# A planner's costs, latencies and transfer model are exchanged in a gated linear attention + mixture-of-experts kernel

## Chip, cores, metric

One core of a Trainium2 chip. The metric is the device time of one execution in microseconds, as the median of several runs.

## What is computed

Two stages. The first is a gated linear attention over 4 batches, 8 heads, 768 steps and 48 features; the second is a mixture of 4 experts over its 3072 x 384 output.

```python
f = 1.0 / (1.0 + np.exp(-f_logit))
for t in range(768):
    state = f[:, :, t, :, None] * state + np.einsum('bhd,bhe->bhde', k[:, :, t], v[:, :, t])
    y[:, :, t] = np.einsum('bhd,bhde->bhe', q[:, :, t], state)
x = y.transpose(0, 2, 1, 3).reshape(3072, 384)
p = domain_probs / (domain_probs.sum(-1, keepdims=True) + 1e-09)
for e in range(4):                                  # w1[e]: 384 x 1024, w2[e]: 1024 x 384
    out += p[:, e:e + 1] * (np.maximum(x @ w1[e], 0.0) @ w2[e])
```

## The kernel before

**Tiling.** The 768 steps are cut into 6 slices (c = 0 to 5) of 128 steps. A slice holds 4 batch blocks (b), so 512 rows of x. Each slice goes through attention (per block) and then through the four experts (per slice).

**Attention of one block.** The steps, by the names that the planner gives them: `gate1` and `gate2` (ACT, L247 and L251: exp and ln of the gate's logits; two blocks at a time from slice 1 on); `cs` (PE, L255: running sum over time with a triangular matrix; in slice 0 also four one-column matmuls, L258); `exps` (ACT, L262 and L264: exp of the negative and of the positive sum, and in slice 0 the small `egs`, L266); `q` and `k` (L276: products with those exps, on DVE or POOL); `v` (a cast, L216 or L218). Then q and k are turned: in slices 0 and 1 by PE transposes (`tpq`, `tpk`, L285) and one PSUM copy (`ev_tp`, ACT or DVE), from slice 2 on by a DMA transpose (`tp`, L289). `at` (PE, L300) makes the scores, `ev_at0` and `ev_at1` (DVE, L304) mask them, `y` (PE, L311 and L315) applies them to v and to the state, `ev_y` copies the result, and `xt` turns it into the transposed input xT of the experts (slices 0 and 1: PE, L340, and a copy `ev_xt`; later: DMA, L293). `kv`, `ev_kv`, `state` (L321, L328, L335) carry the state to the next slice.

**Experts of one slice.** Eight `h` units for each expert (L344, three matmuls of 512 columns each), each followed by a `relu` (ACT L352 or DVE L350), and eight `o` units (L356, four matmuls of 384 columns), every second followed by an eviction `ev_o` (L363, L365 or L367). The h units of expert e are interleaved with the o units of expert e - 1. In slice 1 the first two experts are done in two halves of the rows (blocks 0 and 1, then 2 and 3), so that the first half can begin when its two blocks are there. The h units of slice 0 need all four blocks' xT and the first weight; from slice 2 on all four blocks of the slice's xT.

**Transfers.** Loads of q, k, v and f and all stores, transposes and small `egs` copies are issued by SP, in one order. The eight weight transfers (768 KB each) are issued by POOL (L229). Two waits are written out by hand: the first weight waits until the last k block of slice 0 has landed (L231), and the first load of slice 1 waits until the sixth weight (index 5) has landed (L225).

**What sets the order.** The kernel's text does not give an order of instructions. Each step is an `Op` with a cost for every engine that could do it, a priority, the steps that it depends on, and the buffers that it takes and frees. `Plan.run` (L58) plays the whole program in advance: whenever an engine is free, it takes the step of the best (lowest) priority whose inputs are ready and whose buffers can be had. Engines are asked in the order PE, ACT, DVE, POOL, DMA. The instructions are then emitted in the order of that play, so the plan fixes which engine does a step and what stands before it in each engine's queue; the waits in the program itself come from the data, not from the plan. A step is ready (L46) at the latest of its inputs' ends plus their `lag`, plus `LATENCY` if the input was made on another engine, or 0.05 if on the same one. Buffers are counted in `rooms` (L134): among them four PSUM banks for the experts and four for attention, three `e` buffers for the exps. "DMA" is one row in the plan: a load of one block holds it for 1.05 us, a weight for 4.5 us, and the data is there `lag` (2.0) later.

Priorities: slice 0's loads -1000 and up, weight issues -500 and up, slice 1's loads -400 and up, attention of slice 0 -200 + 3.6 b + 0.8 s with s the step's place in the chain (L501), expert units 0, 1, 2 ... in their order, relus 3 less than their unit, and attention of the next slice between the units (base + 2 + 5 b + s, L537). After the play, PE's idle time before the first h unit is filled with matmuls on a constant tile (`pad`, L551 and L556), one for each 0.2 us of idle time.

Of the kernel before, what the change touches and what calls it, by code (L numbers as in the profile page):

```python
# [14 lines left out]
class Op:  # L15


    def __init__(self, name, costs, emit, prio, deps=(), takes=(), frees=(), lag=0.0):
        self.name, self.costs, self.emit, self.prio = name, costs, emit, prio
        self.deps = [d for d in deps if d is not None]  # L20
        self.takes, self.frees, self.lag = list(takes), list(frees), lag
        self.end = self.start = self.engine = None
        self.pad = 0


class Plan:


    LATENCY = 0.2

    def __init__(self, rooms):
        self.ops, self.rooms = [], {r: list(range(n)) for r, n in rooms.items()}
        self.slot, self.left = {}, {}

# [23 lines left out]
    def run(self):  # L58
        for o in self.ops:
            for k in o.frees:  # L60
                self.left[k] = self.left.get(k, 0) + 1
        left = sorted(self.ops, key=lambda o: o.prio)
        free_at = {e: 0.0 for o in left for e in o.costs}
        free_at.update({"DMA": 0.8, "DVE": 5.0, "POOL": 3.5, "ACT": 2.1, "PE": 2.0})
        freeing, done, now = [], [], 0.0
        while left:
            for f in [f for f in freeing if f[0] <= now + 1e-9]:
                freeing.remove(f)
                self.rooms[f[1]].append(f[2])
            for e in ("PE", "ACT", "DVE", "POOL", "DMA"):  # L70
                while free_at[e] <= now + 1e-9:
                    for o in left:
                        if e in o.costs:
                            t = self.ready(o, e)
                            if t is not None and t <= now + 1e-9 and self.take(o):
                                break
                    else:
                        break
                    left.remove(o)
                    o.engine, o.start, o.end = e, now, now + o.costs[e]  # L80
                    free_at[e] = o.end
                    for k in o.frees:
                        self.left[k] -= 1
                        if self.left[k] == 0:
                            freeing.append((o.end + self.LATENCY, k[0], self.slot[k]))
                    done.append(o)
            nexts = [t for t in free_at.values()] + [f[0] for f in freeing]
            for o in left:
                for e in o.costs:
                    nexts.append(self.ready(o, e) or 0.0)  # L90
            nexts = [t for t in nexts if t > now + 1e-9]
            if left and not nexts:
                raise RuntimeError("no step can run: " + ", ".join(o.name for o in left[:8]))
            if left:
                now = min(nexts)
        return done
# [3 lines left out]
def kernel(  # L100
# [120 lines left out]
    def load(c, nm, b, n):  # L221
        ins[c, nm, b] = nc.sync.dma_start(out=tl(nm, c, b // 2)[:, hh(b, n), :],  # L222
                                          in_=srcs[nm][c, :, b * H:(b + n) * H, :])
        if (c, nm, b) == (1, "f", 0):
            after(ins[c, nm, b], ins["w", 5])  # L225
# [34 lines left out]
    def exps(c, b):  # L260
        cs, e = tl("cs", c, b), tl("e", c, b)
        nc.scalar.activation(out=e[:, 0].rearrange("t (d h) -> t h d", d=D), in_=cs[:, 0:HD].rearrange("t (i r d) -> t r i d", r=2, d=D),  # L262
                             func=AF.Exp, scale=-1.0)
        nc.scalar.activation(out=e[:, 1], in_=cs[:, 0:HD], func=AF.Exp)  # L264
        if c == 0:
            nc.scalar.activation(out=tl("egs", c, b), in_=cs[0:MP, HD:HD + NP], func=AF.Exp, scale=-1.0)  # L266
# [107 lines left out]
    ld = {}  # L374
    nw = [(0, 1), (1, 1), (0, 2), (2, 1), (1, 2), (3, 1), (2, 2), (3, 2)]

    def add_load(c, nm, b, n, prio, deps=()):
        op = P.add(f"ld {nm}{c}.{b}", {"DMA": 1.05 * n}, lambda e: load(c, nm, b, n), prio,
                   deps=deps, takes=[(nm, c, b // 2)], lag=2.0)
        for i in range(n):  # L380
            ld[c, nm, b + i] = op
        return op
# [4 lines left out]
    for i, (e, which) in enumerate(nw):  # L387
        iss = P.add(f"w issue {i}", {"POOL": 0.9}, lambda _, i=i, e=e, which=which: load_w(i, e, which),
                    -500 + i, deps=[ld[0, "k", B - 1]])
        wd[e, which] = wd[i] = P.add(f"w {i}", {"DMA": 4.5}, lambda _: None, -500 + (0, 1, 2, 3, 4, 5, 101.5, 103.5)[i], deps=[iss], lag=2.0)  # L390
    for half in range(2):
        for j, nm in enumerate("fkqv"):
            add_load(1, nm, 2 * half, 2, -400 + 4 * half + j, deps=[wd[5]])
# [4 lines left out]
    def attention(c, slot, gran):  # L398
# [10 lines left out]
        for b in range(B):  # L409
# [6 lines left out]
                       deps=[G[b]], takes=[pt_("cs")], lag=0.2, frees=[("gp", c, half)])  # L416
            ex = P.add(f"exps {c}.{b}", {"ACT": 0.98 if c else 1.1}, on(exps), s(0) + 0.1, deps=[cs],
                       takes=[("e", c, b)] + ([("egs", c, b)] if c == 0 else []), frees=[pt_("cs")])
            GS.append(P.add(f"egs {c}.{b}", {"DMA": 1.0}, on(dma_egs), s(3), deps=[ex], takes=[("egs", c, b)],
                            frees=[("e", c, b)], lag=2.0) if c and more else None)  # L420
            pe = {"DVE": 0.6, "POOL": 1.0} if c < 2 else {"POOL": 1.0}
            qm = P.add(f"q {c}.{b}", pe, one(product, 0), s(4) - 0.2,
                       deps=[ex, ld[c, "q", b]], takes=[("qk", c, b)], frees=[("q", c, half), ("e", c, b)])
            km = P.add(f"k {c}.{b}", pe, one(product, 1), s(4) - 0.1,
                       deps=[ex, ld[c, "k", b]], takes=[("qk", c, b)], frees=[("k", c, half), ("e", c, b)])
            vb = P.add(f"v {c}.{b}", {"ACT": 0.52, "DVE": 0.36} if c == 0 else {"POOL": 0.5, "ACT": 0.52} if c == 1 else {"POOL": 0.5}, one(cast_v), s(4),
                       deps=[ld[c, "v", b]], takes=[("vb", c, b)], frees=[("v", c, half)])
            if c < 2:
                tq = P.add(f"tpq {c}.{b}", {"PE": 0.22}, on(pe_tp, 0), s(4), deps=[qm],
                           takes=[pt_("tp")], frees=[("qk", c, b)], lag=0.2)  # L430
                tk = P.add(f"tpk {c}.{b}", {"PE": 0.22}, on(pe_tp, 1), s(4) + 0.01, deps=[km],
                           takes=[pt_("tp")], frees=[("qk", c, b)], lag=0.2)
                et = P.add(f"ev_tp {c}.{b}", {"DVE": 0.69, "ACT": 1.05}, lambda e, b=b: copy(e, tl("QK", c, b)[0:MP], tl("tp", c, b)), s(4) + 0.1,
                           deps=[tq, tk], takes=[("QK", c, b)], frees=[pt_("tp")])
            else:
                et = P.add(f"tp {c}.{b}", {"DMA": 1.8}, on(dma_tp), s(4), deps=[qm, km], takes=[("QK", c, b)],
                           frees=[("qk", c, b)], lag=2.2)
            at = P.add(f"at {c}.{b}", {"PE": 0.35}, on(pe_at), s(7), deps=[et],
                       takes=[pt_("A", 0), pt_("A", 1)], lag=0.2, frees=[("QK", c, b)])
# [3 lines left out]
                      takes=[pt_("y")], frees=[("QK", c, b), ("AT", c, b), ("vb", c, b)], lag=0.2)  # L443
# [4 lines left out]
            if c < 2:  # L448
                xt = P.add(f"xt {c}.{b}", {"PE": 0.17}, on(pe_xt), s(13), deps=[ey],
                           takes=[pt_("xp")], frees=[("yb", c, b)], lag=0.2)  # L450
                xdone[c, b] = P.add(f"ev_xt {c}.{b}", {"ACT": 0.48, "DVE": 0.4},
                                    lambda e, b=b: copy(e, tl("xT", c)[:, :, b * T:(b + 1) * T], tl("xp", c, b)),
                                    s(13) + 0.1, deps=[xt], takes=[("xT", c)], frees=[pt_("xp")])
            else:
                xdone[c, b] = P.add(f"xt {c}.{b}", {"DMA": 0.9}, on(dma_xt), s(13), deps=[ey], takes=[("xT", c)],
                                    frees=[("yb", c, b)], lag=2.2)
            X.append(xdone[c, b])
        for b in range(B if more else 0):
# [4 lines left out]
                       takes=[pt_("KV")], frees=[("vb", c, b), ("qk", c, b)], lag=0.2)  # L463
# [9 lines left out]
    def add_h(c, e, fc, n0, n1, xs):  # L473
# [3 lines left out]
                  deps=[wd[e, 1]] + [xdone[c, b] for b in xs], takes=[key], lag=0.2, frees=[("xT", c)])  # L477
# [5 lines left out]
    def add_o(c, e, nt, half):  # L483
# [8 lines left out]
                                  deps=d + [wd[e, 2], omm.get((c, e, nt))], takes=[key], lag=0.2, frees=[("h", c, e)])  # L492
        if half == 1 or by_cols:
# [4 lines left out]
            if e == E - 1:  # L498
                P.add(f"store {c}.{nt}.{part}", {"DMA": 0.6}, lambda _: store(c, nt, cols), p, deps=[ev], frees=[("o", c, nt)])
# [20 lines left out]
    for c in range(C):  # L520
        u0 = unit[0]
        pl = P.add(f"ld p{c}", {"DMA": 0.5}, lambda e, c=c: load_p(c), -900 if c == 0 else u0 - 6, lag=2.0)
# [15 lines left out]
        if c + 2 < C:  # L538
            for half in range(2):
                for j, nm in enumerate("fkqv"):  # L540
                    add_load(c + 2, nm, 2 * half, 2, u0 + 30 + 4 * half + j)
# [49 lines left out]
```

## Time and profile before

| what | value |
|---|---|
| median of 3 runs | 304.89 us (304.5, 304.89, 315.0) |
| the profiled execution, its own time | 304.54 us |
| its span in the profile | 302.7 us |
| granted TensorE clock, mean | 0.999 |
| PE busy | 293.2 us |
| ACT / DVE / POOL busy | 170.8 / 138.1 / 95.5 us |
| start of the first L344 matmul (expert stage of slice 0) | 22.74 us |
| HBM read / written | 31.51 / 4.72 MB |

The profile is of one execution; PE's busy time is a union of overlapping matmul records, so it tells that PE had work, not how fast it went. PE is TensorE's matmuls, PEld its weight loads, DVE VectorE, ACT ScalarE, POOL GpSimd, SP SyncE, SPq the issuing of DMAs on SP. A line of the timeline or of the chain gives a start and a duration in us, then engine, line of the code, output and input. The bracket behind it is the idle time of that engine before the instruction, and what ended it.

### The profile page before, as it was taken

To read this page: it belongs to the slowest core of one execution; us is meant where nothing else is said; L and a number is where in the kernel's file an instruction comes from. 1 tells how busy PE (TensorE), PEld (TensorE's weight loads), DVE (VectorE), ACT (ScalarE), POOL (GpSimd) and SP (SyncE) were. 2 spreads that over 40 slices of the span, in tenths; PEclk is the share of its full clock that TensorE was granted. 3 is DMA by queue.
4 is the path that set the end of the run, shared out by engine and by line. 5 is a ranking of instruction groups with operands and counts; after the bars stand their busy time and mean duration, and the time that the engine had idled before them with its cause. 6 is when DMAs were issued, how large, how long until landed. Compare 5 with 4: busy or idle time off the path is not lost.

```text
span 302.7 us, 5517 instructions
## 1 busy us (share of the span) xinstructions
PE 293.2 (97%) x2112; PEld 169.4 (56%) x2143; DVE 138.1 (46%) x273; ACT 170.8 (56%) x295; POOL 95.5 (32%) x157
## 2 busy tenths in 40 slices
PE   7899999999999999999999999999999999999995
PEld 5565555567775655455555555555555555555553
DVE  6774013787853764516555344544423443201223
ACT  5767654857865444676356475345566344475440
POOL 4584400409656237423426143522332100000000
PEclk9999999999999999999999999999999999999999
DMA  7999999954994589866997877301322201100003
GB/s 157 203 193 204 207 206 193 228 83 91 217 207 84 111 161 187 189 122 120 182 187 134 216 142 147 56 13 28 100 61 51 48 14 30 67 22 2 0 0 106
DMA packets 137355, 36.10 MB, mean 119 GB/s; under 512 B 128496, under 2 KB 135792, under 8 KB 137328
## 3 DMA queue, kind: packets, MB, share of 16 engines
q1 hardware_dynamic: 131568, 29.45, 49.1%
q0 software_dynamic: 5760, 6.29, 12.4%
q8 instruction: 17, 0.28, 0.4%
q14 instruction: 10, 0.08, 0.1%
HBM read 31.51 MB, written 4.72 MB: 120 GB/s over the span
## 4 chain that ended last, share of the span: by engine, by line
PE 88%; DMA 4%; DVE 2%; SPq 2%; issue 1%; POOL 1%; ACT 1%; DVEq 0%; ACTq 0%; POOLq 0%
PE ps_m L356 41%; PE ps_m L344 40%; DMA w_sb<-in_moe_w_dram 3%; PE ps_t L300 2%; SPq L222 2%; DMA f<-in_f_logit_dram 1%; PE ps_t L315 1%; PE ps_t L321 1%; PE ps_t L311 1%; PE ps_t L255 1%; PE ps_t L285 1%; DVE qk L276 1%; POOL qk L276 0%; DVE AT L304 0%; POOL Sf L335 0%
## 5 line engine op out<-in xcount | busy, mean ns | idle before, releaser
L352 ACT ACTIVATE h<-ps_m 128x512 bf16<-128x512 f32 (+1 forms) x171 | 98.3, 577 | 103.0 <-PE ps_m L344 92.9
L356 PE MATMUL ps_m<-w_sb,h 128*128 128x384 bf16 x776 | 153.0, 324 | 0.2
L344 PE MATMUL ps_m<-xT,w_sb 128*128 128x512 bf16 (+1 forms) x593 | 150.4, 362 | 2.1 <-DVE o L367 0.3
L356 PEld LDWEIGHTS <-h 128*128 128x128 bf16 x776 | 73.0, 98 | 57.0
L363 DVE SCALAR_TENSOR_TENSOR o<-ps_m,pn,o 128x384 f32<-128x384 f32 (+1 forms) x73 | 44.6, 611 | 96.8 <-PE ps_m L356 89.4
L344 PEld LDWEIGHTS <-w_sb 128*128 128x128 bf16 x624 | 59.8, 98 | 47.1 <-issue 0.7
L276 POOL TENSOR_TENSOR qk<-q,e 128x384 bf16<-128x384 f32 x19 | 22.8, 1204 | 64.9 <-ACT e L262 64.4
L304 DVE TENSOR_TENSOR AT<-ps_t,mask 128x512 bf16<-128x512 f32 x48 | 31.1, 683 | 19.2 <-PE ps_t L300 19.1
L335 POOL TENSOR_TENSOR Sf<-Sf,egs 48x192 f32<-48x192 f32 x40 | 20.4, 510 | 48.8 <-DVE Sf L328 46.8
L350 DVE TENSOR_SCALAR h<-ps_m 128x512 bf16<-128x512 f32 (+1 forms) x37 | 20.7, 572 | 22.0 <-PE ps_m L344 19.8
L276 POOL TENSOR_TENSOR qk<-k,e 128x384 bf16<-128x384 f32 x20 | 21.0, 1052 | 19.8 <-ACT e L264 12.9
L262 ACT ACTIVATE e<-ps_t 128x384 f32<-128x384 f32 x24 | 20.7, 864 | 3.7 <-PE ps_t L255 2.4
L328 DVE TENSOR_TENSOR Sf<-Sf,ps_t 48x192 f32<-48x192 f32 x40 | 14.0, 349 | 6.1 <-PE ps_t L321 5.3
L336 POOL CAST sb<-Sf 48x192 bf16<-48x192 f32 x40 | 13.6, 339 | 2.6
L365 ACT ACTIVATE o<-ps_m,pn 128x384 f32<-128x384 f32 x20 | 11.6, 580 | 3.9 <-PE ps_m L356 3.1
L264 ACT ACTIVATE e<-ps_t 128x384 f32<-128x384 f32 x24 | 13.0, 541 | 0.0
L556 PE MATMUL ps_m<-busy 128*128 128x256 bf16 x71 | 11.5, 301 | 1.3 <-DVE busy L140 1.3
L218 DVE CAST yb<-ps_t 128x384 bf16<-128x384 f32 x16 | 8.9, 555 | 7.4 <-PE ps_t L315 6.3
L247 ACT ACTIVATE ex<-f 128x768 f32<-128x768 f32 (+1 forms) x14 | 10.5, 748 | 3.1 <-DMA f<-in_f_logit_dram 2.9
L315 PE MATMUL ps_t<-vb,AT 128*128 128x48 bf16 x192 | 11.4, 184 | 0.7 <-DVE vb L218 0.7
L315 PEld LDWEIGHTS <-AT 128*128 128x128 bf16 x192 | 9.8, 97 | 3.0 <-issue 1.0
L251 ACT ACTIVATE gp<-ex 128x768 bf16<-128x768 f32 (+1 forms) x14 | 10.5, 751 | 0.4
(50 smaller groups left out, 139.9 us busy)
## 6 DMA issues: line engine op xcount, KB each, us to landing
w_sb<-in_moe_w_dram POOLq DMA_DIRECT2D x8, 768.0 KB, 18.8
out_dram<-o SPq DMA_DIRECT2D x23, 192.0 KB, 2.1
f<-in_f_logit_dram SPq DMA_DIRECT2D x10, 384.0 KB, 4.3
k<-in_k_dram SPq DMA_DIRECT2D x10, 384.0 KB, 5.2
q<-in_q_dram SPq DMA_DIRECT2D x10, 384.0 KB, 5.3
v<-in_v_dram SPq DMA_DIRECT2D x10, 384.0 KB, 5.5
f<-in_f_logit_dram SPq DMA_DIRECT2D x4, 192.0 KB, 4.0
k<-in_k_dram SPq DMA_DIRECT2D x4, 192.0 KB, 4.0
```

The costliest lines, as they stand in the source:

```text
L262: nc.scalar.activation(out=e[:, 0].rearrange("t (d h) -> t h d", d=D), in_=cs[:, 0:HD].rearrange("t (i r d) -> t r i d", r=2, d=D), func=A ...
L276: engines[eng].tensor_tensor(out=tl("qk", c, b)[:, j, :, 0:D].rearrange("t (i r) d -> t i r d", r=2), in0=tl("qk"[j], c, b // 2)[:, hh(b), ...
L304: nc.vector.tensor_tensor(out=tl("AT", c, b)[:, r].rearrange("s i t -> s (i t)"), in0=tl("A", c, b, r).rearrange("s i t -> s (i t)"), in1= ...
L315: nc.tensor.matmul(out=y[:, h * D:(h + 1) * D], lhsT=AT[:, r, i, :], rhs=vb[:, h, :], start=(c == 0), stop=True, skip_group_check=True)
L328: nc.vector.tensor_tensor(out=Sf[rows, b], in0=Sf[rows, b], in1=KV[rows, :, r, :], op=ALU.add)
L335: nc.gpsimd.tensor_tensor(out=Sf[rows, b], in0=Sf[rows, b], in1=eg, op=ALU.mult)
L336: nc.gpsimd.tensor_copy(out=nb[rows, b, :, r * D:(r + 1) * D], in_=Sf[rows, b])
L344: nc.tensor.matmul(out=tl("hp", c, e, fc, n0)[:, n0:n1], lhsT=w1_sb[:, e, kk, fc * 128:(fc + 1) * 128], rhs=tl("xT", c)[:, kk, n0:n1], sta ...
L350: nc.vector.tensor_relu(out=dst, in_=src)
L352: nc.scalar.activation(out=dst, in_=src, func=AF.Relu)
L356: nc.tensor.matmul(out=tl("op", c, e, nt, part)[:, cols], lhsT=tl("h", c, e)[:, fc, nt * T:(nt + 1) * T], rhs=w2_sb[:, e, fc, cols], start ...
L363: nc.vector.scalar_tensor_tensor(out=o, in0=op, scalar=pe, in1=o, op0=ALU.mult, op1=ALU.add)
```

## The change

No computation, buffer or transfer is added or removed, and the two waits written out by hand stay as they are. What changes is the play that sets the order:

- `LATENCY` goes from 0.2 to 0.07, and the `lag` of every PE step from 0.2 to 0.05. A step may be taken up to `AHEAD` = 0.06 us before it is ready (it then starts when it is ready).
- Transfers on SP get a model of a ring: a DMA costs its issue time on "DMA" (0.6 for a load, 1.2 to 1.25 for two `egs` copies or a transpose, 0.45 for a store), its data passes through one `ring` in order (1.0 for a block, 0.1 to 0.6 for the others), the issue is held back when the ring is more than 4.0 us behind, and the data is there 1.6 us after its turn in the ring.
- The weights leave "DMA" and get a row "W" of their own, in the order of issue, each 4.5 us, `lag` 1.5.
- In the plan slice 1's loads depend on weight 7 instead of weight 5, and the loads of slice c + 2 on the last v load of slice c + 1.
- `exps` becomes two steps (`exps0`, `exps1`) of 0.88 and 0.54 us (0.72 in slice 0) in place of one of 0.98 (1.1 in slice 0); `q` depends on the first, `k` on the second, `egs` on the first.
- Costs: products 0.7 on DVE and 1.2 or 1.1 on POOL (0.6 and 1.0 before); DVE is free from 5.2 on (5.0).

The diff, its core (the same `lag=0.2` to `0.05` edit is left out where it is repeated):

```diff
-    LATENCY = 0.2
+    LATENCY, AHEAD = 0.07, 0.06
...
-        free_at.update({"DMA": 0.8, "DVE": 5.0, "POOL": 3.5, "ACT": 2.1, "PE": 2.0})
+        free_at.update({"DMA": 0.8, "DVE": 5.2, "POOL": 3.5, "ACT": 2.1, "PE": 2.0})
...
-            for e in ("PE", "ACT", "DVE", "POOL", "DMA"):
+            for e in ("PE", "ACT", "DVE", "POOL", "DMA", "W"):
...
-                            if t is not None and t <= now + 1e-9 and self.take(o):
+                            if t is not None and t <= now + self.AHEAD and self.take(o):
...
-                    o.engine, o.start, o.end = e, now, now + o.costs[e]
+                    o.engine, o.start = e, max(now, t)
+                    o.end = o.start + o.costs[e]
+                    if o.ring is not None:
+                        self.ring = max(self.ring, o.end) + o.ring
+                        o.end = max(o.end, self.ring - 4.0)
+                        o.lag = self.ring - o.end + 1.6
...
-                            freeing.append((o.end + self.LATENCY, k[0], self.slot[k]))
+                            freeing.append((o.end + (self.LATENCY if o.ring is None else o.lag), k[0], self.slot[k]))
...
-    def exps(c, b):
+    def exps(c, b, j):
         cs, e = tl("cs", c, b), tl("e", c, b)
-        nc.scalar.activation(out=e[:, 0].rearrange("t (d h) -> t h d", d=D), in_=cs[:, 0:HD].rearrange("t (i r d) -> t r i d", r=2, d=D),
-                             func=AF.Exp, scale=-1.0)
-        nc.scalar.activation(out=e[:, 1], in_=cs[:, 0:HD], func=AF.Exp)
-        if c == 0:
+        if j == 0:
+            nc.scalar.activation(out=e[:, 0].rearrange("t (d h) -> t h d", d=D), in_=cs[:, 0:HD].rearrange("t (i r d) -> t r i d", r=2, d=D),
+                                 func=AF.Exp, scale=-1.0)
+        else:
+            nc.scalar.activation(out=e[:, 1], in_=cs[:, 0:HD], func=AF.Exp)
+        if j == 1 and c == 0:
             nc.scalar.activation(out=tl("egs", c, b), in_=cs[0:MP, HD:HD + NP], func=AF.Exp, scale=-1.0)
...
-        op = P.add(f"ld {nm}{c}.{b}", {"DMA": 1.05 * n}, lambda e: load(c, nm, b, n), prio,
-                   deps=deps, takes=[(nm, c, b // 2)], lag=2.0)
+        op = P.add(f"ld {nm}{c}.{b}", {"DMA": 0.6}, lambda e: load(c, nm, b, n), prio,
+                   deps=deps, takes=[(nm, c, b // 2)], ring=1.0 * n)
...
-        wd[e, which] = wd[i] = P.add(f"w {i}", {"DMA": 4.5}, lambda _: None, -500 + (0, 1, 2, 3, 4, 5, 101.5, 103.5)[i], deps=[iss], lag=2.0)
+        wd[e, which] = wd[i] = P.add(f"w {i}", {"W": 4.5}, lambda _: None, -500 + i, deps=[iss], lag=1.5)
...
-            add_load(1, nm, 2 * half, 2, -400 + 4 * half + j, deps=[wd[5]])
+            add_load(1, nm, 2 * half, 2, -400 + 4 * half + j, deps=[wd[7]])
...
-            ex = P.add(f"exps {c}.{b}", {"ACT": 0.98 if c else 1.1}, on(exps), s(0) + 0.1, deps=[cs],
-                       takes=[("e", c, b)] + ([("egs", c, b)] if c == 0 else []), frees=[pt_("cs")])
-            GS.append(P.add(f"egs {c}.{b}", {"DMA": 1.0}, on(dma_egs), s(3), deps=[ex], takes=[("egs", c, b)],
-                            frees=[("e", c, b)], lag=2.0) if c and more else None)
-            pe = {"DVE": 0.6, "POOL": 1.0} if c < 2 else {"POOL": 1.0}
+            ex = [P.add(f"exps{j} {c}.{b}", {"ACT": (0.88, 0.54 if c else 0.72)[j]}, on(exps, j), s(0) + 0.1 + 0.1 * j, deps=[cs],
+                        takes=[("e", c, b)] + ([("egs", c, b)] if c == 0 else []), frees=[pt_("cs")]) for j in range(2)]
+            GS.append(P.add(f"egs {c}.{b}", {"DMA": 1.2}, on(dma_egs), s(3), deps=[ex[0]], takes=[("egs", c, b)],
+                            frees=[("e", c, b)], ring=0.1) if c and more else None)
+            pe = {"DVE": 0.7, "POOL": 1.2} if c < 2 else {"POOL": 1.1}
...
-                et = P.add(f"tp {c}.{b}", {"DMA": 1.8}, on(dma_tp), s(4), deps=[qm, km], takes=[("QK", c, b)],
-                           frees=[("qk", c, b)], lag=2.2)
+                et = P.add(f"tp {c}.{b}", {"DMA": 1.25}, on(dma_tp), s(4), deps=[qm, km], takes=[("QK", c, b)],
+                           frees=[("qk", c, b)], ring=0.5)
...
-                xdone[c, b] = P.add(f"xt {c}.{b}", {"DMA": 0.9}, on(dma_xt), s(13), deps=[ey], takes=[("xT", c)],
-                                    frees=[("yb", c, b)], lag=2.2)
+                xdone[c, b] = P.add(f"xt {c}.{b}", {"DMA": 1.2}, on(dma_xt), s(13), deps=[ey], takes=[("xT", c)],
+                                    frees=[("yb", c, b)], ring=0.2)
...
-                P.add(f"store {c}.{nt}.{part}", {"DMA": 0.6}, lambda _: store(c, nt, cols), p, deps=[ev], frees=[("o", c, nt)])
+                P.add(f"store {c}.{nt}.{part}", {"DMA": 0.45}, lambda _: store(c, nt, cols), p, deps=[ev], frees=[("o", c, nt)], ring=0.6)
...
-        pl = P.add(f"ld p{c}", {"DMA": 0.5}, lambda e, c=c: load_p(c), -900 if c == 0 else u0 - 6, lag=2.0)
+        pl = P.add(f"ld p{c}", {"DMA": 0.6}, lambda e, c=c: load_p(c), -900 if c == 0 else u0 - 6, ring=0.5)
...
-                    add_load(c + 2, nm, 2 * half, 2, u0 + 30 + 4 * half + j)
+                    add_load(c + 2, nm, 2 * half, 2, u0 + 30 + 4 * half + j, deps=[ld[c + 1, "v", B - 1]])
```

## The prediction

> **What bounds the kernel now.** I read the page's busy line and chain first, then the chain of waits in order of time, then the timeline of the first 70 us engine by engine.
>
> ```profile
> span 302.7 us, 5517 instructions
> ...
> PE 293.2 (97%) x2112; PEld 169.4 (56%) x2143; DVE 138.1 (46%) x273; ACT 170.8 (56%) x295; POOL 95.5 (32%) x157
> ...
> PE 88%; DMA 4%; DVE 2%; SPq 2%; issue 1%; POOL 1%; ACT 1%; DVEq 0%; ACTq 0%; POOLq 0%
> ```
>
> The chain is PE for 88% of the span. In order of time it is PE from 22.74 us on; before that it is a weight transfer, released by a load:
>
> ```profile
> 13.03 1.36 POOL qk L276
> 14.38 0.25 issue
> 14.63 8.07 DMA w_sb<-in_moe_w_dram
> 22.70 0.05 issue
> 22.74 0.39 PE ps_m L344
> ```
>
> So the first MoE matmul (call it the start) waits for the first weight, issued 0.3 us after the last k block landed (14.32). But the other input, slice 0's xT, is ready only just before it. The timeline shows where its last block's (b=3) products were made:
>
> ```profile
> 13.53 0.55 ACT L264 ACTIVATE e<-ps_t 128x384 f32<-128x384 f32 x1
> ...
> 15.72 0.54 DVE L276 TENSOR_TENSOR qk<-k,e 128x384 bf16<-128x384 f32 x1
> 16.18 0.84 DVE L276 TENSOR_TENSOR qk<-q,e 128x384 bf16<-128x384 f32 x1
> ...
> 21.96 0.48 ACT L216 COPY xT<-ps_t 128x384 bf16<-128x384 bf16 x1 [0.73 <-PE ps_t L340]
> 22.74 0.98 PEld L344 LDWEIGHTS <-w_sb 128*128 128x128 bf16 x6 [0.55 <-DMA w_sb<-in_moe_w_dram]
> ```
>
> xT is whole at 22.44: cover of 0.3 us, no more. From the end of the products (17.02) to xT it took 5.42 us.
>
> After the start PE is nearly perfect: a unit (three L344 or four L356 matmuls) goes every 0.65 us. From the matmuls' start times I count two real holes, about 0.25 us at 69.55 and 0.5 us at 80.89. Slice 1 is the tight place. Its first load waits for the sixth weight and its chain runs from 52.29 to 66.76:
>
> ```profile
> 42.16 0.37 SPq L222 DMA_DIRECT2D f<-in_f_logit_dram  x1
> ```
>
> ```profile
> 52.29 0.84 ACT L247 ACTIVATE ex<-f 128x768 f32<-128x768 f32 x1 [1.30 <-DMA f<-in_f_logit_dram]
> ...
> 66.28 0.48 ACT L216 COPY xT<-ps_t 128x384 bf16<-128x384 bf16 x1 [1.62 <-PE ps_t L340]
> ```
>
> PE runs out of slice 0's units at 69.2, so slice 1's first half had 2.4 us to spare.
>
> **The change part by part.** No instruction is added or removed; each engine's order changes. The most to be won is therefore little: the start cannot pass the first weight (at most the 0.3 us between landing and issue), and behind it there are 0.75 us of holes. I follow the planner's rule by hand from the costs in the code to learn the order, and price that order with durations of the trace.
>
> *The start.* By the new costs slice 0's exps take 0.88+0.72 us on ACT where one step took 1.1; the trace has 0.87, 0.53 and 0.16 overlapping, about 1.25 in all. As two steps they can be parted, and ACT is asked before DVE. Working it through: ev_tp of b=0 goes to ACT (ready 8.53, ACT free 8.48; it was on DVE), so b=1's exps start at 9.58. v of b=0 goes to ACT at 14.32. POOL takes b=2's q at 14.39, then at 15.59 the eight weight issues (ready 15.07, best priority), planned to 22.79, so POOL is shut for b=3's products. exps1 of b=3 is set behind ev_xt of b=0, ev_tp of b=2 and v of b=2, to about 18.6; a near tie at 16.92 could put it at 16.9. Either way DVE gets k of b=3 behind the two masks of b=2, whose priority is better.
>
> Priced with the trace: on ACT, b=0's ev_tp runs 8.15 to 9.2 (1.02 us). Behind it wait b=1's exps, and for them POOL's and DVE's products. ev_tp of b=2 ends near 17.3; v of b=2 landed at 17.18 and is cast by 17.7 (0.51); exps1 of b=3 ends near 18.2, against 14.08. The masks of b=2 follow at about 18.0 to 19.3 (0.64 each), then k (0.54) to 19.8. With the same 5.42 us behind it xT is whole at 25.2: 25.2 - 22.74 = **+2.5 us**. Bounds: -0.3 (issue gap) and +3.5 (a PSUM bank still held by b=1's y when b=2's scores want two adds 0.6, a worse mix of copies 0.4). I take +2.5, the row-by-row sum. Nothing hides it: the weight's cover ends at 22.7 to 22.9.
>
> *Slice 1's loads.* In the plan they now depend on the eighth weight instead of the sixth; on SP they still wait only for the sixth (the wait in the load function is untouched), so data will land as before, f at 52.27. But ACT, DVE and PE get slice 1's steps where the plan has them. Before: loads and weights in one DMA row, 0.8 + 16 x 1.05 + 0.5 = 18.1, seven weights to 49.6, f's 2.1 and 2.2 to land: 53.9, for a start worked out at 25.05: 28.9 us after it. New: W begins at about 16.5, eight times 4.5 is 52.5, +1.57, +0.6 issue, +2.0 ring, +1.67: f at 58.4 for a start worked out at 26.2 in the same way, 32.2 after it. That is 3.3 us later in PE's stream. Against it six PE hand-overs in the chain cost 0.12 planned instead of 0.4 and six hand-overs back 0.07 instead of 0.2, 2.5 us less, with the dearer exps +0.9: net 1.6 less. Chain later by 1.7 us, spare 2.4: **0**. If the cover goes, it costs what exceeds 2.4. The second half gains: its f was planned 41.8 us after the start and is 40.2 now, so I let most of the 0.75 us of holes go: **-0.5** (bounds -0.75 and 0). Late next is then PE itself.
>
> The trace shows weights and loads sharing engines: that f took 10.1 us from issue to landing where the page's median is 4.3, and the eighth weight landed 5.25 us after the seventh, where the third to seventh came every 3.6 to 4.4. [...]
>
> *Tighter hand-overs.* From an h unit's first matmul to its relu the trace has 0.85 us (35.21 to 36.06): 0.645 + 0.205, planned 0.12 now, 0.4 before. A step chosen at its very first moment makes PE wait up to 0.1; with moments spread over a 0.65 us unit that is 0.1 x 0.1 / 1.3, 0.008 us a step, for some 300 steps at most 2 us, but PSUM banks and slots leave most of them room: **+0.2** (0 to 2).
>
> *Slices 2 to 5.* Attention there follows its slots; xT landed 2 to 3 us ahead of need (slice 4: 205.57 against about 208). DMA transposes are planned shorter (3.35 against 4.2 us), slice 2's loads at about 72 as before (71.23 in the trace). **0** (0 to +1). The tail behind the last matmul (299.6 to 302.7) keeps its instructions: 0.
>
> Sum: +2.5 + 0 - 0.5 + 0.2 = +2.2. The profiled execution ran 304.54 us (span 302.7 and 1.8 around it), 0.35 below the median of 304.89; 304.54 + 2.2 = 306.7, as a median 307.0.
>
> **The rivals.**
> 1. *The start stays, slice 1 stalls.* If b=3's products come in time, the start is at 22.8 and planned near 22.1; f at 57.9 is then 35.8 after it, 7 later than before, less 1.6, less the 2.4 spare: PE stands still for 3 us near 69, less 0.5: about 307. For: the plan's own arithmetic; against: POOL is shut when b=3 needs it.
> 2. *Nothing shows.* Products under the weight's cover and slice 1 within its spare: 304.5 less 0 to 0.75, 304.0 to 304.9. For: real loads land up to 1 us before the plan has them. Against: cover of 0.3 us.
> 3. *Slower by over 2%.* One mechanism: slice 1's chain, whose place PE meets near 69. The chain took 14.5 us; planned 35.8 after the start with no shortening it ends 50.3 after it, at 73.0; with POOL products (1.2 us where DVE has 0.54 to 0.84) and the two ev_tp on ACT in a row (2.1) ahead of both halves, 76 or more. It decides once slice 1's first h unit comes later than 69.2 + 6.1 = 75.3. Price 6.5 us and up: 311.5 to 314. Against: the chain is shortened in the plan, and once PE stands still nothing competes with it.
>    No hole in this trace is longer than 0.75 us and the granted clock stays at 1.00, so no row prices a cold restart. [...]
>
> **How the numbers follow.** Late start 0.48 (306 to 308.5); rival 1 0.17 (305.5 to 308); rival 2 0.16; rival 3 0.17; a gain over 2%, which would need the start before 17 us, 0.02. The likeliest gives 307.0. From 304.0 to 311.0 leaves out rival 3 and the 0.02: 0.19. Two per cent of 304.89 is 6.1 us, about what a measurement of this kernel can tell from no change: faster 0.02, same 0.81, slower 0.17.
>
> **What would show it.** Right: the first L344 matmul near 25 us, released by ACT's xT copy instead of the weight; on DVE the last k product behind b=2's masks near 19.5; POOL's weight issues near 14.7; ACT's first 128x768 exp (slice 1) later than 52.3, though f lands there; no hole at 80.9. Wrong: a start at 22.7, or a hole of several us near 69, or holes of 0.1 us all along PE's row.

## Result and profile after

The changed kernel takes 318.88 us in the median (4 runs, 318.09 to 319.6), the kernel before 305.14 beside it: ratio 1.046 (1.0425 to 1.0495). The profiled execution took 319.42 us, its span is 317.6. The sign is that of rival 3; its place is not. Of most kernels here, the kernel before among them, some runs are 5 to 13 us longer than the rest; the ratios leave out every run that is more than 1.5% above the fastest of its kernel.

From the page after, its busy line, its chain and the granted clock in 40 slices of the span:

```profile
span 317.6 us, 5524 instructions
...
PE 299.0 (94%) x2119; PEld 171.9 (54%) x2150; DVE 137.8 (43%) x273; ACT 170.7 (54%) x296; POOL 94.6 (30%) x156
...
PEclk9999999999999879999999999999999999999999
...
PE 82%; DMA 5%; issue 4%; DVE 4%; ACT 2%; POOL 2%; SPq 0%; POOLq 0%; DVEq 0%; ACTq 0%
```

The span is 14.9 us longer, PE busy only 5.8 longer, so PE stood still for the other 9.1; and the clock row has a dip at its 14th and 15th slice, about 103 to 119 us.

The start is where the prediction put it. The timeline after, 18 to 25 us:

```profile
18.32 1.29 DVE L312 TENSOR_TENSOR AT<-ps_t,mask 128x512 bf16<-128x512 f32 x2
...
19.52 0.55 DVE L284 TENSOR_TENSOR qk<-k,e 128x384 bf16<-128x384 f32 x1
...
24.73 0.48 ACT L222 COPY xT<-ps_t 128x384 bf16<-128x384 bf16 x1 [0.43 <-PE ps_t L348]
```

The last k product stands behind b=2's masks on DVE, and the first L352 matmul begins at 25.26, released by xT: 2.5 us later than the 22.74 of before. The exact figure is chance in part: four other traces below have the same plan up to there and begin at 24.61 to 26.01.

The rest is behind it. The timeline of PE after, the scores' matmuls (`at`, L308) of slice 2's blocks 1 to 3 and of block 2 of slice 3; the bracket is PE's idle time and what ended it:

```profile
95.16 0.40 PE L308 MATMUL ps_t<-QK 48*128 48x128 bf16 x8 [1.54 <-DMA QK<-qk]
105.62 0.40 PE L308 MATMUL ps_t<-QK 48*128 48x128 bf16 x8 [1.24 <-DMA QK<-qk]
109.61 0.61 PE L308 MATMUL ps_t<-QK 48*128 48x128 bf16 x8 [2.84 <-DMA QK<-qk]
...
156.96 0.40 PE L308 MATMUL ps_t<-QK 48*128 48x128 bf16 x8 [2.08 <-DMA QK<-qk]
```

PE waits for a DMA transpose of QK (SP issues it; PE needs its output for the scores), five times and 8.2 us in all (the fifth, 0.55, is at 165.08). In the kernel before the same list of waits has no line of QK between 82 and 170 us. Around the longest wait PE also runs at half clock, from 108.96 to 115.79 (granted 0.50): the 46 matmuls recorded from 109.61 to there take 6.2 us, where their columns need 3.1 at the pace of the same trace at clock 1.00 (four matmuls of 384 columns, or three of 512, in 0.65 us, 117.20 to 118.49). Windows of the profile after (us, PE, PEld, DVE, ACT, POOL busy, granted clock, DMA share, GB/s):

```profile
109.00:112.50 3.50, 2.89 (x25) 1.71 (x26) 0.85 (x2) 0.60 (x1) 0.63 (x2) 0.50 1.08 217
112.50:116.00 3.50, 3.28 (x24) 2.09 (x24) 1.79 (x5) 0.79 (x2) 1.69 (x5) 0.53 1.03 204
116.00:119.00 3.00, 3.00 (x22) 1.71 (x20) 2.31 (x5) 2.27 (x4) 1.66 (x5) 1.00 0.70 141
```

**Where the 14.9 us lie.** The last matmul ends at 314.53 (before: 299.61), the tail behind it is 3.1 us in both. From the first L352 matmul to the last end both traces record the same 1913 matmuls; I summed each one's distance to the next less its columns' time at full clock (that same pace), by stretch:

| us | more than before | what |
|---|---|---|
| start | +2.5 | 22.74 to 25.26 |
| to 82 | +0.9 | slice 1: two holes, 1.06 at 72.3 and 0.62 at 78.0 |
| 82 to 119 | +8.1 | slice 2: three waits for QK, 6.1 from start to start; half clock and a 0.6 in it, 2.0 |
| 119 to 162 | +1.9 | slice 3: 2.25 at 154.5 |
| 162 to the end | +1.4 | slice 3: 0.7 at 164.2; the rest in pieces under 0.24 |

**The queue that made it.** SP issues in the plan's order. The plan (from playing the kernel's own text) and the trace after, by start of issue and landing:

| step | plan | trace |
|---|---|---|
| first load of slice 3 (f) | 93.28 | 96.23 |
| QK transpose of b=2, slice 2 | 95.88, there 101.98 | 100.96, there 105.57 |
| QK transpose of b=3, slice 2 | 99.53, there 102.88 | 106.31, there 109.56 |
| QK transposes of b=2, b=3, slice 3 | there 144.68, 151.48 | there 156.92, 165.03 |

Queue of SP, timeline after:

```profile
96.23 1.80 SPq L228 DMA_DIRECT2D f<-in_f_logit_dram  x1
98.09 1.14 SPq L228 DMA_DIRECT2D k<-in_k_dram  x1
99.27 1.57 SPq L228 DMA_DIRECT2D q<-in_q_dram  x1
100.96 2.66 SPq L297 DMA_TRANSPOSE QK<-qk  x1
103.72 2.49 SPq L301 DMA_TRANSPOSE xT<-yb  x2
106.31 1.25 SPq L297 DMA_TRANSPOSE QK<-qk  x1
```

and the same place before:

```profile
96.95 0.59 SPq L222 DMA_DIRECT2D f<-in_f_logit_dram  x1
...
102.60 2.93 SPq L289 DMA_TRANSPOSE QK<-qk  x2
...
106.89 1.61 SPq L222 DMA_DIRECT2D k<-in_k_dram  x1
```

Two things are to be read here. Before, slice 2's two last QK transposes stood ahead of slice 3's k and q; after, k and q stand ahead. And yet the data is there no later: those two transposes landed at 105.67 and 109.09 before and at 105.57 and 109.56 after. Before, PE's order had their matmuls at 107.65 and 109.39, behind expert units enough to fill the time, and without a wait:

```profile
107.65 0.40 PE L300 MATMUL ps_t<-QK 48*128 48x128 bf16 x8
109.39 0.40 PE L300 MATMUL ps_t<-QK 48*128 48x128 bf16 x8
```

The old plan had these two landings at 109.20 and 111.00, 2 to 4 us later than they came; its error was on the safe side. After, the matmuls stand further forward among the units, for landings planned at 101.98 and 102.88, and PE stands still with units still to do behind them. The new plan frees SP 0.6 us after a load (1.4 for q, which the ring holds back) and 1.25 after a transpose; the trace has 1.14 to 1.80 and up to 2.66. So in slice 2 the plan's queue runs 3 to 7 us ahead of the real one, and PE, ordered by the plan, comes to L308 before the data.

### The profile page after: what moved, and what is told of

It is laid out like the page before. It is cut to its first block, busy times and chain, and to the rows that moved or that the text cites. A ratio compares the mean times of both kernels' runs of the same rounds, so it can differ in the third digit from the quotient of the medians.

```text
span 317.6 us, 5524 instructions
## 1 busy us (share of the span) xinstructions
PE 299.0 (94%) x2119; PEld 171.9 (54%) x2150; DVE 137.8 (43%) x273; ACT 170.7 (54%) x296; POOL 94.6 (30%) x156
## 4 chain that ended last, share of the span: by engine, by line
PE 82%; DMA 5%; issue 4%; DVE 4%; ACT 2%; POOL 2%; SPq 0%; POOLq 0%; DVEq 0%; ACTq 0%
PE ps_m L364 37%; PE ps_m L352 36%; DMA QK<-qk 3%; PE ps_t L308 2%; POOL qk L284 1%; PE ps_t L323 1%; PE ps_t L261 1%; PE ps_t L329 1%; DVE AT L312 1%; PE ps_t L293 1%; DVE qk L284 1%; PE ps_t L319 1%; PE ps_m L564 1%; DMA f<-in_f_logit_dram 1%; ACT e L269 1%
## 5 line engine op out<-in xcount | busy, mean ns | idle before, releaser
L364 PE MATMUL ps_m<-w_sb,h 128*128 128x384 bf16 x776 | 155.4, 325 | 0.3
L352 PE MATMUL ps_m<-xT,w_sb 128*128 128x512 bf16 (+1 forms) x593 | 153.4, 364 | 2.2 <-DVE o L371 0.5
L352 PEld LDWEIGHTS <-w_sb 128*128 128x128 bf16 x624 | 60.1, 98 | 45.8 <-issue 1.8
L284 POOL TENSOR_TENSOR qk<-q,e 128x384 bf16<-128x384 f32 x20 | 24.0, 1202 | 82.6 <-ACT e L269 80.3
L343 POOL TENSOR_TENSOR Sf<-Sf,egs 48x192 f32<-48x192 f32 x40 | 21.3, 532 | 28.6 <-DVE Sf L336 26.7
L224 POOL CAST vb<-v 128x384 bf16<-128x384 f32 x18 | 9.8, 556 | 35.5 <-PE ps_t L329 19.5
L284 POOL TENSOR_TENSOR qk<-k,e 128x384 bf16<-128x384 f32 x18 | 17.9, 996 | 5.6 <-ACT e L272 5.6
L308 PE MATMUL ps_t<-QK 48*128 48x128 bf16 x192 | 9.6, 222 | 9.5 <-DMA QK<-qk 8.2
L564 PE MATMUL ps_m<-busy 128*128 128x256 bf16 x78 | 14.5, 322 | 1.3 <-DVE busy L146 1.3
L308 PEld LDWEIGHTS <-QK 48*128 48x128 bf16 x192 | 5.5, 95 | 18.0 <-DMA QK<-qk 10.7
L375 DVE TENSOR_SCALAR o<-ps_m,pn 128x384 f32<-128x384 f32 x6 | 3.7, 618 | 21.2 <-PE ps_m L364 21.2
```

Of the source, the lines that this page charges most:

```text
L284: engines[eng].tensor_tensor(out=tl("qk", c, b)[:, j, :, 0:D].rearrange("t (i r) d -> t i r d", r=2), in0=tl("qk"[j], c, b // 2)[:, hh(b), ...
L308: nc.tensor.matmul(out=tl("A", c, b, r)[:, i, :], lhsT=QK[rows, 1, i, :], rhs=QK[rows, 0, i, :], start=True, stop=True)
L343: nc.gpsimd.tensor_tensor(out=Sf[rows, b], in0=Sf[rows, b], in1=eg, op=ALU.mult)
L352: nc.tensor.matmul(out=tl("hp", c, e, fc, n0)[:, n0:n1], lhsT=w1_sb[:, e, kk, fc * 128:(fc + 1) * 128], rhs=tl("xT", c)[:, kk, n0:n1], sta ...
L364: nc.tensor.matmul(out=tl("op", c, e, nt, part)[:, cols], lhsT=tl("h", c, e)[:, fc, nt * T:(nt + 1) * T], rhs=w2_sb[:, e, fc, cols], start ...
L564: nc.tensor.matmul(out=spare[:, 0:256], lhsT=busy[:, 0:128], rhs=busy, start=True, stop=True)
```

## Experiments

Ratios are taken against the kernel before, run beside it on the same chip. Each kernel has one trace.

**Which part of the change.** Four kernels: one part alone, or all but one part.

*latency_only*: the kernel before with the hand-over times (and DVE free from 5.2).

```diff
-    LATENCY = 0.2
+    LATENCY, AHEAD = 0.07, 0.06
-        ... lag=0.2
+        ... lag=0.05
```

> The kernel before with the shorter latencies alone (LATENCY 0.07, AHEAD 0.06, lag 0.05, DVE free from 5.2). If the loss comes from the transfer model (theory 1), this one has none of it: first L344 matmul at 22.7 to 23.0, no hole on PE over 1 us, within 1 us of before. If tight hand-overs are the cause (theory 2), PE waits appear all along and it is 6 to 12 us slower than before.

Measured: 316.86, 316.75, 314.38 and 310.83 us, ratio 1.023 (1.0157 to 1.0303). The trace is of the 316.86: its first large matmul comes only at 32.44 (see the last section), and from there to the last one it takes 279.6 us, before 276.9. No wait for QK between 82 and 170 us; six holes of 0.35 to 1.0 us between 66 and 93. Neither expectation came whole: alone it is not free, but what it costs is not what the changed kernel loses in slices 2 and 3.

*two_exps_only*: the kernel before with exp as two steps.

```diff
-            ex = P.add(f"exps {c}.{b}", {"ACT": 0.98 if c else 1.1}, on(exps), ...
+            ex = [P.add(f"exps{j} {c}.{b}", {"ACT": (0.88, 0.54 if c else 0.72)[j]}, on(exps, j), ...
```

> The kernel before with exp as two steps alone (new step costs, latencies and transfers as before). By theory 1 it moves only the start: ACT's second exps of the last block go behind other copies and the first L344 matmul comes at 24.5 to 27, with slices 2 and 3 free of holes, 2 to 4 us slower than before. If the split is innocent, within 1 us of before.

Measured: 308.3 us in one run, 316.31 to 317.79 in the other three, which have no trace. In the traced run, the 308.3, PE waits for no QK; the first large matmul is at 27.68, a little behind the 24.5 to 27 of the theory and 4.9 us later than before, and 1.2 of this is won back behind it. So a late start alone does not throw slices 2 and 3 out of step.

*one_exps*: the changed kernel with exp as one step again (the diff above, reversed).

> The changed kernel with exp as one step again (its cost of before); latencies and the transfer model stay. By theory 1 the start goes back to 22.7 to 23.5 and the holes before L308 in slices 2 and 3 stay: 2 to 3 us faster than the changed kernel, 11 to 13 slower than before. If the late start is what throws slices 2 and 3 out of step, it is within 2 us of before.

Measured: 320.25 us, ratio 1.0486 (1.046 to 1.0511). It was to be 2 to 3 us faster than the changed kernel and is 1.4 slower. The first large matmul is at 24.07, 1.2 us earlier than in the changed kernel; the loss behind it stays:

```profile
PE ps_t L306 <- DMA QK<-qk: 7.9, 5, 2.9
```

(us in total, times, longest; 82 to 170 us; its L306 is L308.) From the first large matmul to the last it takes 1.8 us more than the changed kernel (two stretches at half clock, from 105.88 and from 163.91; granted clock of the traced run 0.988 in the mean). So the split is not needed for the loss in slices 2 and 3; the 1.2 us at the start is of the size of the spread between equal starts.

*old_transfers*: the changed kernel with all transfers modelled as before.

```diff
-            for e in ("PE", "ACT", "DVE", "POOL", "DMA", "W"):
+            for e in ("PE", "ACT", "DVE", "POOL", "DMA"):
...
-        op = P.add(f"ld {nm}{c}.{b}", {"DMA": 0.6}, ..., ring=1.0 * n)
+        op = P.add(f"ld {nm}{c}.{b}", {"DMA": 1.05 * n}, ..., lag=2.0)
...
-            add_load(1, nm, 2 * half, 2, -400 + 4 * half + j, deps=[wd[7]])
+            add_load(1, nm, 2 * half, 2, -400 + 4 * half + j, deps=[wd[5]])
```

> The changed kernel with the transfers planned as before (loads 1.05 a block on one row with the weights, old costs and lags, slice 1 behind weight 5, no dependency of a slice's loads on the slice before's); shorter latencies and split exps stay. By theory 1 the waits of PE for QK transposes in slices 2 and 3 vanish and what stays is the start at 24 to 25.5: 1.5 to 3.5 us slower than before. By theory 2 it stays 10 us or more slower.

Measured: 307.94 and 308.52 us, ratio 1.0087 (1.0056 to 1.0117); 317.88 and 318.84 in the other two. The trace is of the 318.84 (its start is late, at 35.52, see the last section), and no line of QK is left in it between 82 and 170 us. The transfer model carries the loss of slices 2 and 3.

*ring_only*: the other way round, the kernel before with the transfer model alone (the diff above, reversed, on the kernel before, and the dependency of a slice's loads on those of the slice before).

> The kernel before with only the transfer model of the change in its plan (weights on a queue of their own, the ring, the new issue times, slice 1's loads behind the eighth weight, a slice's loads behind those of the slice before); its hand-over times, its DVE and POOL costs and its one exp step stay. Theory, the transfer model with its issue times that are too short is what costs slices 2 and 3, whatever the rest of the plan: holes over 1 us before the QK^T matmuls of slices 2 and 3, last matmul 10 us or more behind its plan (301.1), 312 to 320 us. Rival, it takes the tighter hand-overs as well: no such holes, 304 to 308 us.

Measured: 321.33 us (320.29 to 322.26, and one run of 329.23), ratio 1.0506 (1.0448 to 1.0565), a little above the range of the theory. Last matmul 14.4 us behind its plan, and

```profile
PE ps_t L305 <- DMA QK<-qk: 7.0, 6, 2.8
```

Alone it is enough.

**What in the transfer model.** Four edits of the changed kernel, for three explanations: (a) the order on SP, loads ahead of transposes; (b) the planned landing of the transposes; (c) slice 1's loads planned behind the eighth weight.

*loads_behind*: a slice's loads behind the last xT transpose of the slice before.

```diff
-    ... deps=[ld[c + 1, "v", B - 1]])
+    ... deps=[ld[c + 1, "v", B - 1], xdone[c + 1, B - 1] if c else None])
```

> The changed kernel with one more dependency: the loads of slices 3 to 5 stand behind the last xT transpose of the slice before, so on SP no load of slice 3 stands ahead of slice 2's QK transposes. Theory (a), the order on SP is what makes PE wait before L308 in slices 2 and 3: the holes of 1.7, 1.4 and 3.0 us of slice 2 go, with them the stretch at half clock, and those of slice 3 as well; 307 to 311 us. Theory (b), the planned landing is too early whatever stands ahead: more than half of the wait stays, 315 us or more. Theory (c), it comes of slice 1's loads standing behind the eighth weight: no change, 318 to 320.

Measured: 310.93 us (310.64 to 311.17, and one run of 321.7), ratio 1.0165 (1.0132 to 1.0198). The queue of SP and, in the list of waits between 82 and 170 us, all that PE waits for:

```profile
97.57 1.73 SPq L297 DMA_TRANSPOSE QK<-qk  x1
...
102.01 1.25 SPq L297 DMA_TRANSPOSE QK<-qk  x1
...
110.05 0.58 SPq L228 DMA_DIRECT2D f<-in_f_logit_dram  x1
```

```profile
PE ps_t L308 <- DMA QK<-qk: 1.8, 1, 1.8
```

One added dependency takes 8 us off. Only the wait at 94 us is left, for a transpose that no load of slice 3 stands ahead of; slice 3 has none, and the granted clock stays at 1.00. This is what (a) expected, but for that one wait.

*late_transposes*: the plan lands the transposes of slices 2 and 3 3 us later.

```diff
-                        o.lag = self.ring - o.end + 1.6
+                        o.lag = self.ring - o.end + (4.6 if o.name.startswith(('tp 2', 'tp 3')) else 1.6)
```

> The changed kernel, in whose plan the QK transposes of slices 2 and 3 land 3 us later than before; nothing else in the plan is changed. Theory (b), the plan's landing is too early and PE comes to L308 before the data: the holes before L308 in slices 2 and 3 shrink to under 1 us each, no half clock there; 307 to 311 us. Theory (a), the order on SP: the transposes still stand behind the loads and land 3 to 7 us later than planned, of which 3 are now covered: about half of the loss goes, 312 to 315. Theory (c): no change, 318 to 320.

Measured: 318.32 us (one run 324.94), ratio 1.0403 (1.0356 to 1.045): no gain, which neither (a) nor (b) had. Only (c) had this number, and w5 below speaks against (c). The wait moved. PE between 82 and 170 us:

```profile
PE ps_m L352 <- ACT h L360: 3.9, 5, 1.2
PE ps_t L308 <- DMA QK<-qk: 3.2, 3, 1.2
PE ps_m L352 <- DMA xT<-yb: 0.9, 1, 0.9
```

The waits for QK shrink to 3.2 us and the half clock goes (granted 1.00 from 82 to 162 us), but now all four loads of slice 3's first half stand ahead of the transpose (it is issued at 102.88 and lands at 107.34, later than in the changed kernel), and the experts run short instead: their L352 matmuls wait 3.9 us for relus on ACT and 0.9 for xT. A later landing time in the plan does not mend the queue.

*issue_times*: SP held as long as the trace shows; the ring, and all else, stays.

```diff
-        op = P.add(f"ld {nm}{c}.{b}", {"DMA": 0.6}, ...
+        op = P.add(f"ld {nm}{c}.{b}", {"DMA": 1.5 if c else 0.6}, ...
-            GS.append(P.add(f"egs {c}.{b}", {"DMA": 1.2}, ...
+            GS.append(P.add(f"egs {c}.{b}", {"DMA": 2.2}, ...
-                et = P.add(f"tp {c}.{b}", {"DMA": 1.25}, ...
+                et = P.add(f"tp {c}.{b}", {"DMA": 1.9}, ...
```

> The changed kernel, in whose plan SP is held as long as the trace of the changed kernel shows: 1.5 us for a load behind slice 0 (0.6 before), 2.2 for the pair of g stores (1.2), 1.9 for a QK transpose (1.25); the ring stays. Theory (b) in its narrow form, the short issue times alone let SP's queue run 3 to 7 us ahead of the real one: the holes of slices 2 and 3 go, 307 to 312 us, last matmul near its planned 302.1. If instead the ring is what is wrong: holes over 1 us stay before L308, 314 to 320.

Measured: 309.19 and 309.37 us (317.06 and 319.85 in the other two), ratio 1.0114 (1.0072 to 1.0156). Between 82 and 170 us PE waits once, 0.3 us, for a relu; no QK. Last matmul 304.39, 2.3 behind its plan. Three numbers take off 9.6 us, and the ring itself is not at fault. The queue of SP in its trace:

```profile
102.76 1.23 SPq L297 DMA_TRANSPOSE QK<-qk  x1
...
107.09 1.24 SPq L297 DMA_TRANSPOSE QK<-qk  x1
108.39 0.58 SPq L228 DMA_DIRECT2D f<-in_f_logit_dram  x1
...
113.13 0.57 SPq L228 DMA_DIRECT2D k<-in_k_dram  x1
```

With longer issue times the plan itself puts slice 3's loads behind slice 2's last QK transpose again, and it has that transpose at 108.43, no longer too early (107.09). So this edit mends the order of (a) and the times of (b) together and does not part them; both come from the issue times.

*w5*: slice 1's loads planned behind the sixth weight again.

```diff
-            add_load(1, nm, 2 * half, 2, -400 + 4 * half + j, deps=[wd[7]])
+            add_load(1, nm, 2 * half, 2, -400 + 4 * half + j, deps=[wd[5]])
```

> The changed kernel with one edit: slice 1's loads stand behind the sixth weight, as in the kernel before, not behind the eighth. Theory (c), that the late loads of slice 1 push slice 2's transfers together: slice 1's holes (1.9 us) go and so do those of slices 2 and 3, 306 to 311 us. Theories (a) and (b): only the 1.2 us of slice 1 goes, the holes before L308 in slices 2 and 3 stay, 315 to 319.

Measured: 322.1 us (320.21 to 324.09), ratio 1.0534 (1.0449 to 1.0619), above every range. The waits for QK stay (5.8 us, five times), so (c) falls, and the edit adds a loss. The plan has slice 1's f at 49.3; it lands at 53.2. Timeline, ACT and PE:

```profile
53.22 0.84 ACT L253 ACTIVATE ex<-f 128x768 f32<-128x768 f32 x1 [4.88 <-DMA f<-in_f_logit_dram]
```

```profile
54.99 0.48 PE L261 MATMUL ps_t<-gp,Ub 128*128 128x384 bf16 x2 [4.03 <-ACT gp L257]
```

An error of the same kind in another place: f goes out when the sixth weight has landed (43.08; the plan has 45.06), beside the last two weights, and takes 10.1 us from issue to landing, where the ring, which knows nothing of the weights, gives it 4.2. So `cs` stands in PE's order 4 us before its data. The dependency on the eighth weight hides that error in the changed kernel.

**Towards a better plan.**

*tuned_plan*: the changed kernel with one exp step, the times of issue_times, slice 1's loads behind the sixth weight, and the weights issued behind the last q load instead of the last k load.

```diff
-                    -500 + i, deps=[ld[0, "k", B - 1]])
+                    -500 + i, deps=[ld[0, "q", B - 1]])
```

> The changed kernel with exp as one step again, the issue times on SP as measured (1.5, 2.2 and 1.9 us), slice 1's loads behind the sixth weight, and the weights issued once the q load of the last quarter has landed instead of the k load. Theory: with SP's queue planned as it runs, the transposes land in time, and with the loads of slice 1 early its holes go too; the start is 24.1 to 24.5 us against 22.7 of the kernel before, the plan ends at 297.7 against 299.9: 302 to 306 us. Rival, a transfer model with a ring can't be made to keep SP in step: holes before L308 stay, 308 to 318.

Measured: 309.95 us, ratio 1.0145 (1.0125 to 1.0164): it misses the theory's 302 to 306. No wait for QK is left, as the theory has it, but the start is at 24.40 (1.7 later than before), `cs` of slice 1 waits 1.9 us for its gate at 54.6, and the transposes on PE near 60 us stand 1.7 us for their products. No kernel here beats the one before.

*before_early_w* and *before_late_w*: the kernel before with its weights issued behind another q load (the diff above with `"q", B - 2` and `"q", B - 1`).

> The kernel before, with the weights issued once the third q load of slice 0 has landed, some 2 us earlier than behind the last k load. Theory, a load of slice 0 that is issued beside or behind the first weight lands only 12 to 16 us later, as the last v load did in the trace of the kernel with the old transfer plan (issued 14.07, landed 30.03, first weight issued 14.86): here the last two v loads are issued behind the first weight in every run, PE stands still some 8 to 10 us near 20 us, and every run takes 312 to 320 us. Rival, the late v load was an accident of the chip in that run: the first weight lands 2 us earlier and the time is 303 to 306.

> The kernel before, with the weights issued once the last q load has landed, some 0.8 us later than behind the last k load. Same theory: the last v load is always issued a clear 1 us ahead of the first weight and lands in 5 us; the start of the first large matmul goes from 22.7 to 23.5 us, the time from 305.4 to 306, and no run takes over 308. Rival, accident: one run in four still takes 312 to 316.

Measured: the early one 305.72 to 317.15 us in 10 runs, ratio 1.0032 (0.9968 to 1.0096). It tells nothing, since the edit did not do what it was meant to: the wait that is written out by hand still holds the first weight until the last k block has landed, and it was issued at 15.03 in the trace, not earlier than before (14.63). POOL stood idle for it:

```profile
15.03 3.35 POOL L229 DMA_DIRECT2D w_sb<-in_moe_w_dram  x4 [2.92 <-DMA k<-in_k_dram]
```

The late one: 306.19 to 310.64 in 10 runs, ratio 1.0051 (1.0007 to 1.0095); 2 of its 10 runs over 308, where the kernel before, beside it, had 8 of 19 over 308 and up to 318.27. That speaks for the theory that the load and the weight collide and does not prove it: those two runs (308.87 and 310.64) are above the 308 that it allowed. The trace is of the 308.87: its last v load landed in 4.9 us, but the first weight took 9.7 (8.1 before), PE stood still for it until 25.09, and half clock followed until 27.83 (granted clock of the run 0.994 in the mean).

## Why the prediction was wrong, point by point

- **The start, +2.5: right**, in size (25.26 against 25.2) and in mechanism (k of b=3 on DVE at 19.52 behind b=2's masks at 18.32, xT the releaser). That it agrees to 0.1 us is luck, with equal starts between 24.61 and 26.01. Which edits make it was not taken apart: without the split it is 24.07 (one_exps), and the transfer model alone, without the split, has 24.32 (ring_only).
- **Slice 1's loads, 0, and -0.5 for the holes: wrong by 1.4.** ACT took the first 128x768 exp at 57.22 though f landed at 52.90, as the signpost said; the spare of 2.4 us did not quite hold it, and two holes of 1.06 and 0.62 came in place of those that went (in w5, without the later dependency, neither is there). The later dependency has two sides: with it f lies unused for 4.3 us; without it (w5) f is 10.1 us on its way beside the last two weights, where the ring gives it 4.2, and PE waits 4.03 us.
- **Tighter hand-overs, +0.2:** not a cost by steps of 0.008 us. Alone they reorder enough to cost 5.4 us in the shortest run of latency_only (2.7 of it behind the start in the one trace, of another run), with six holes of 0.35 to 1.0 us; within the change they cost nothing that shows: ring_only, without them and with one exp step, is at 321.3, one_exps, with them, at 320.3. The parts do not add up, since each of them changes the order.
- **"Slices 2 to 5 ... 0 (0 to +1)": this is the step that failed.** It measured +11.4 with the half clock in it (8.1, 1.9 and 1.4). The working looked at xT, which had 2 to 3 us to spare, and at slice 2's loads; it named the shorter costs of loads and transposes on SP and did not follow SP's queue with them to where slice 3's loads meet slice 2's QK transposes. It put slice 2's loads "at about 72 as before": 72 is the new plan (72.38), and the old one has 75.40. Played to the end, the old plan has slice 2's four `at` steps at 99.36, 102.69, 109.69 and 111.33, the new one at 92.05, 93.37, 102.37 and 103.37, 7 to 9 us further forward, while the data came at most 1.1 us earlier. QK had no spare at all in the order that came out. The plan was played by hand for the first 60 us, where SP has its short loads (0.45 to 0.98 us each), and there the costs hold; they fail where loads are of two blocks and transposes follow.
- **Rival 3, 0.17:** its sign came, its mechanism did not: PE met slice 1's chain with holes of 1.06 and 0.62 us, not 6. PE did come before its data, but in slices 2 and 3 and through SP. The prediction gave the clock no price, since no row of before had one (granted 0.999 in the mean); here it cost 2 to 3 us (2.0 by the table, which sets it against the small losses of before, 3.1 by the matmuls at half clock), with 0.50 granted from 109 to 112.5 us.
- **Signposts:** the two for the start came (the weight issues, due near 14.7, began at 15.19). None of the three signs of being wrong came either. "No hole at 80.9" came as well and told nothing, since the holes went elsewhere. None of them looked behind 81 us, where the term that failed, slices 2 to 5, had its place.

## What to carry to other kernels

When a planner's costs change, replay every in-order queue to the end of the program, the issuing engine's first of all: issue costs too small by some 1 us each led to no wait of PE for a transpose before 93 us, and the stretch behind it lost 11 us, where a transpose that PE waits for stood behind three loads. How long an issue holds SP is read from its own queue in the trace, under the load in question, not at the start: a load's took 0.45 to 0.98 us in the first 11 us of the changed kernel's trace and 1.14 to 1.80 from 96 to 101. A model that is better in one part (the ring) can lose to a crude one whose errors had been kept apart by longer costs; mend the issue times of the queue that PE waits for first: they set its order and its landings (issue_times, 9.6 us won), where a later landing alone gave nothing (late_transposes).

## What was not expected of the hardware

**Half clock after short holes.** In the changed kernel PE's idle 2.84 us before 109.61 go with 6.83 us at half clock, 108.96 to 115.79 (granted 0.50). In w5 PE waits 4.03 us before 54.99, and the granted clock is 0.57 from 56 to 60 us; between 82 and 170 us its longest wait is 1.8 us (for QK), and yet the clock is 0.51 from 93.8 to 97.3. Other waits of that length had no half clock beside them: 1.8 us in loads_behind (granted 1.00 from 82 to 162), 1.9 in tuned_plan (1.0 in the mean of that run), and 2.08 before 156.96 in the changed kernel (1.00 from 119 to 162).

So in these traces the length of the longest wait does not tell the two cases apart: 1.8 us is in both. What does was not settled.

**A load beside the first weight.** In two traces, old_transfers and latency_only, PE stands still from about 20 us on for a late load (10.46 us before 30.99, and 5.80 before 27.67). From old_transfers, ACT, POOL and SP:

```profile
13.29 3.38 SPq L228 DMA_DIRECT2D v<-in_v_dram  x2
...
14.86 1.70 POOL L235 DMA_DIRECT2D w_sb<-in_moe_w_dram  x2 [0.35 <-DMA k<-in_k_dram]
...
30.05 0.51 ACT L222 CAST vb<-v 128x384 bf16<-128x384 f32 x1 [10.71 <-DMA v<-in_v_dram]
```

The second v load was issued at 14.07, over 2.61 us, while the first weight went out at 14.86, and landed at 30.03, 16 us after its issue; the one ahead of it, issued at 13.29, took 5.1. In latency_only the last v load was issued at 14.63, the first weight at 14.70, and the load landed at 26.76. In the traces of before (14.13 against 14.63) and after (13.29 against 15.19) it landed within 5.1. A short lead does not decide it alone: in ring_only the load led by 0.27 (14.74 against 15.01) and landed in 5.0. Why a load can fall so far behind beside a 768 KB weight transfer was not settled.
